# The first eight rows of both weights as a pipeline with one written order per engine

## The chip, the cores and the metric

The kernel runs on one core of one Trainium2 chip. The core has a tensor engine (PE; its weight loads are listed apart as PEld), a vector engine (DVE), a scalar engine (ACT), GpSimd (POOL) and a sync engine (SP) that issues the transfers here. The metric is the device time of one execution in microseconds; less is better.

## What is computed

Inputs are `x` (8 batches, 8 heads, 512 tokens, 64 features), `state` (8 batches, 8 heads, 32 slots, 64 features) and two weights of a feed-forward part, `w_in` (512 x 2048) and `w_out` (2048 x 512).

```python
scores  = scale * x @ state^T          # per batch and head, 512 x 32
a       = softmax(scores)              # over the 32 slots
xread   = a @ state
scores2 = scale * state @ x^T          # the same numbers, transposed
a2      = softmax(scores2)             # over the 512 tokens
sread   = a2 @ x
X       = concat(xread, sread)         # heads side by side: 4352 rows x 512
h       = X @ w_in
out     = (h - tanh(h)) @ w_out
```

The weights arrive as 64-bit floats (a block of 128 x 512 is 512 KB) and are turned into 32-bit floats on the chip by integer operations.

## The kernel before, in words

**What a chunk is.** A chunk is one batch's 512 token rows (chunk 8 is the 256 rows of `sread`). `xread` is never formed: for a batch `b` the kernel forms a product of the state with `w_in` (called `m`, 256 x 512 for each quarter `q` of the 2048 hidden columns), and a hidden row `f` (128 of the 2048 hidden columns) is `m` times the softmax weights `at`. There are 16 hidden rows per chunk. Each is followed by tanh (ACT, tile `t`), a subtraction (DVE), and a split of the result into two parts of reduced precision, high by an ACT cast and low by a DVE subtraction (tile `g`, L98 and L99, or L631 and L632 at the start). An output row adds the hidden row's share to the chunk's four output banks: 12 matmuls, high x high, high x low, low x high (L459 to L461). A hidden row takes two full-precision matmuls where `m` is not split (L417, two records each), else six of reduced precision (L419 to L421).

**The weights.** A block of `w_in` or `w_out` is loaded raw (L117) into one of five buffers (`parts` x 3 and `twins` x 2, taken in turn, L94), and converted in four steps (L128 to L132): a shift with a mask on DVE, a merge on DVE, a scaled copy of the low word on ACT, and an addition on DVE. `w_out` blocks are then split by ACT and DVE into the tile `wo` (L244). `w_in` is also written back to memory in 32 bits (`wf`, L519, L608) for the products of later batches. `load(n)` issues the next n loads of the list at L522; in most places it is called behind a conversion, which frees a buffer.

**Order of chunks.** Chunk 0 does its first 8 rows, then chunk 1 does all 16, then chunk 0 its last 8 (with the first half's sum kept in memory, `half`), then chunks 2 to 8. This is the list `steps`; the loop over it takes the hidden row two steps ahead (`LAG`), then the output row of the step itself. `SCH` says at which step a piece of conversion, of a product pair or of another batch's attention is put in.

**What sets the order on the engines.** At the start a written string, `SEQ`, gives one order for all engines: `D` blank matmuls, `S` scores, `c T M B E Z N A` the softmax of batch 0 (copy, transpose, maximum, subtraction, exp, sum with its reciprocal, multiplication, transpose back), `a r b p` the four conversion steps of a column block of `w_in`, `m` its product, `k` and `R` the copies of that product for batch 0 and batch 1, `h H` the two halves of a hidden row, `X` tanh with its subtraction, `G` the split. It covers the first quarter's four columns and two hidden rows. Everything behind that, from the second quarter of `w_in` (as four row blocks, products at L165) and the first `w_out` block on, is ordered by the compiler's own planner, which works from estimated times; `issue_after` gates hold a piece back until a given instruction has been issued.

**Banks and buffers.** PSUM has four output banks (`ps_o`), two for hidden rows (`ps_h`), two for products and scores (`ps_a`). `t` and `g` have three buffers each, `wor` and `cr` (converted block, scaled low word) two.

Of the kernel before, what the change touches and what calls it, by code (L numbers as in the profile page):

```python
# [19 lines left out]
P = 128  # L20
# [16 lines left out]
def attention_ffn(ctx: ExitStack, tc: tile.TileContext, xT, xn, bd, bh, sp, sm, sl, win, wout, xout, sout):  # L37
# [34 lines left out]
    wo = cpool.tile([P, NFF, 2, DM], F32R, name="wo")  # L72
# [21 lines left out]
    raws = itertools.cycle([parts] * PB + [twins] * 2)  # L94
# [6 lines left out]
    class Weight:  # L101
# [17 lines left out]
        def steps(self, dst):  # L119
# [5 lines left out]
            r = pool.tile([P, 512], I32, tag="cr", name=f"{self.name}r", bufs=CB)  # L125
# [115 lines left out]
    def convert_wout(f, part):  # L241
        w = pool.tile([P, 512], F32, tag="wor", name=f"wor{f}", bufs=RB)
        part.convert(w)
        split(wo[:, f, 0], wo[:, f, 1], w)  # L244


    def attention(b, aT):


        if b < LONE:  # L250
            bdr = pool.tile([P, 4, 64], F32, tag="bdr", name=f"bdr{b}", bufs=1)
        else:
            bdr = pool.tile([P, 4, NS], F32, tag="bdr", name=f"bdr{b}", bufs=1)
        with tc.issue_after(loadlog[min(len(loadlog) - 1, XH1)]):
            nc.sync.dma_start(bdr, bd[b] if b < LONE else bh[b - LONE])
# [7 lines left out]
        pss = {}  # L263

        def scores(hf):
            pss[hf] = bank(ps_a, f"sps{b}{hf}")
            for c in range(2):
                nc.tensor.matmul(pss[hf][64 * c : 64 * c + 64], bdr[:, 2 * hf + c], xrs[hf][:, c], start=True, stop=True)

        def all_scores():  # L270

            pss.update({hf: bank(ps_a, f"sps{b}{hf}") for hf in range(2)})
            for j in range(4):
                for hf in range(2):
                    rs = slice(64 * hf, 64 * hf + 64)
                    nc.tensor.matmul(  # L276
                        pss[hf][32 * j : 32 * j + 32], bdr[rs, j], xrs[j // 2][rs, j % 2], start=True, stop=True
                    )

        if b >= LONE:  # L280
            all_scores()
        for hf in range(2):
            if b < LONE:
                scores(hf)
            ps = pss[hf]
            s = pool.tile([P, 512], F32, tag=f"s{b}{hf}" if b < EARLY_S else "s", name=f"s{b}{hf}", bufs=1 if b < EARLY_S else 2)
            nc.scalar.copy(s, ps)
# [11 lines left out]
        for hf in range(2):  # L299
            e = es[hf]  # L300
            ef = e.rearrange("p a n -> p (a n)")
            z = pool.tile([P, 16, 1], F32, tag="z", name=f"z{b}{hf}")
            nc.vector.reduce_sum(z, e, axis=AX.X)
            nc.vector.tensor_scalar_add(z, z, EPS)
            nc.vector.reciprocal(z, z)
            nc.vector.tensor_mul(e, e, z.broadcast_to([P, 16, 32]))
            if b == 1:

                if hf == 0:
                    both = pool.tile([P, 2, 512], F32, tag="x", name="at1", bufs=XB)  # L310
                at = both[:, hf]
            else:
                at = pool.tile([P, 512], F32, tag="at", name=f"at{b}{hf}", bufs=1)
            nc.vector.transpose(at, ef)
            if b == 1:
                ats[1][hf] = at
            if b != 1:
                split(aT[:, 0, hf], aT[:, 1, hf], at)
            yield
        if b == 1:  # L320
            for hf in range(2):
                yield split(aT[:, 0, hf], aT[:, 1, hf], both[:, hf])
        if b >= EARLY_S:
            yield from state_read(b, ss)
        else:
            late[b] = ss

    late = {}

    def late_read(b):  # L330
        yield from state_read(b, late[b])

    def split_first():
        for hf in range(2):
            yield split(aTs[0][:, 0, hf], aTs[0][:, 1, hf], ats[0][hf])
# [57 lines left out]
    class Chunk:  # L393
# [38 lines left out]
        def output(self, f):  # L432
# [17 lines left out]
            if f == NFF - 1 or self.i == 0 and f == HALF - 1:  # L450
# [3 lines left out]
        def add(self, f, t):  # L454
# [4 lines left out]
            nc.tensor.matmul(o, g[:, 0, tok], wo[:, f, 0], start=first, stop=False)  # L459
            nc.tensor.matmul(o, g[:, 0, tok], wo[:, f, 1], start=False, stop=False)  # L460
            return nc.tensor.matmul(o, g[:, 1, tok], wo[:, f, 0], start=False, stop=last).ins  # L461

        def store(self, t, f):
# [15 lines left out]
            if t % 2 == 0:  # L479
# [15 lines left out]
    def advance(units, n=1):  # L495
# [12 lines left out]
    w0[0] = [  # L508
        Weight(win[:, j * P : j * P + P].rearrange("(r p) f -> p r f", p=P), f"w0{j}") for j in range(4)
    ]  # L510
# [3 lines left out]
    def convert_win(q, p):  # L514
# [18 lines left out]
    firstDVE = [None]  # L533

    def o(x):
        tc.keep_in_program_order(x)
        if x.ins.engine == mybir.EngineType.DVE:
            firstDVE[0] = x.ins

    aTs[0] = pool.tile([P, 2, 2, 512], F32R, tag="aT0", name="aT0", bufs=1)  # L540
    bdr = pool.tile([P, 4, 64], F32, tag="bdr", name="bdr0", bufs=1)
    sps = pool.tile([P, 4, P], F32, tag="sm", name="sps", bufs=1)
    xrs = [pool.tile([P, 2, 512], F32, tag="x", name=f"xT0{hf}", bufs=XB) for hf in range(2)]
    load(1)
# [8 lines left out]
    warm = bank(ps_a, "warm")  # L553
    m_first[0] = pool.tile([P, 2, 512], F32, tag="mr", name="mr00", bufs=RRB)
    wb, mps, sps_ps, hps, ss = {}, {}, {}, {}, {}
    es, ms, zs = {}, {}, {}
    csteps = {}
    hts = {}
    PING = int('0')
    tanhs = []  # L560
    nd = 0

    def e3(hf):
        return es[hf].rearrange("p (a n) -> p a n", n=32)

    def step(op):
        k, j = op[0], int(op[1]) if len(op) > 1 else 0
        if k == "D":
            o(nc.tensor.matmul(warm[:, :256], blank[:, :P], blank[:, :256], start=True, stop=True))  # L569
        elif k == "S":  # L570
            sps_ps[j] = bank(ps_o, f"sps0{j}")
            for c in range(2):
                o(nc.tensor.matmul(sps_ps[j][64 * c : 64 * c + 64], bdr[:, 2 * j + c], xrs[j][:, c], start=True, stop=True))
        elif k == "c":
            ss[j] = pool.tile([P, 512], F32, tag=f"s0{j}", name=f"s0{j}", bufs=1)
            o(nc.scalar.copy(ss[j], sps_ps[j]))
        elif k == "T":
            es[j] = pool.tile([P, 512], F32, tag="e", name=f"e0{j}")
            o(nc.vector.transpose(es[j], ss[j]))
        elif k == "M":  # L580
            ms[j] = pool.tile([P, 16, 1], F32, tag="m1", name=f"m10{j}")
            o(nc.vector.reduce_max(ms[j], e3(j), axis=AX.X))
        elif k in "Bq":
            o((nc.gpsimd if k == "q" else nc.vector).tensor_sub(e3(j), e3(j), ms[j].broadcast_to([P, 16, 32])))
        elif k == "E":
            o(nc.scalar.activation(es[j], es[j], AF.Exp, scale=SCALE))
        elif k == "Z":
            zs[j] = pool.tile([P, 16, 1], F32, tag="z", name=f"z0{j}")
            o(nc.vector.reduce_sum(zs[j], e3(j), axis=AX.X))
# [200 lines left out]
```

## Time and profile before

| | us |
|---|---|
| three runs | 669.41, 669.62, 669.88 (median 669.62) |
| span of the profiled execution | 669.9 |
| PE busy | 654.2 |
| PEld busy | 517.9 |
| DVE busy | 458.7 |
| ACT busy | 375.0 |
| POOL busy | 1.2 |

In the profile an instruction row gives its start and length in us, engine, line, operation, output and inputs, form and count, and in brackets the idle time before it with what ended it. Matmuls overlap: the length of one is longer than the distance to the next, so distances between starts, or the net lengths in the chain of waits, are what adds up. A full-precision matmul shows as two records. The granted clock is the share of full speed that PE's clock had. The records begin at 0.24 us with constants; the last transfer is issued at 666.59 us.

### The profile page before, as it was taken

Reading aid. Unit: us, or ns where it says so; the run is one execution under the profiler, and the core shown is the slowest. Engines: PE = TensorE matmul, PEld = TensorE weight load, DVE = VectorE, ACT = ScalarE, POOL = GpSimd, SP = SyncE. Lnnn points to the kernel's source line nnn. Section 1 sums busy time; section 2 is a strip of 40 time slices with the busy share of each in tenths; the row PEclk is TensorE's granted clock in tenths of the full one; section 3 lists DMA queues with packets and bytes.
Section 4 is the critical chain, followed back from the end, with each engine's and each line's share of the span. In section 5 each row is a group of like instructions: output and inputs, shape, how many; then the busy total and the mean of one; then the engine's idle time right before and its main releaser. Section 6 shows DMA issues by size and latency. Waiting matters only on the chain.

```text
span 669.9 us, 9418 instructions
## 1 busy us (share of the span) xinstructions
PE 654.2 (98%) x3452; PEld 517.9 (77%) x3452; DVE 458.7 (68%) x809; ACT 375.0 (56%) x665; POOL 1.2 (0%) x7
## 2 busy tenths in 40 slices
PE   7789999999999999999999999999999999999997
PEld 4446577887888878887888788887878788888996
DVE  5879898968856468667974589457864686444542
ACT  3676587867755555676755566544433454333442
POOL 0000000000000000000000000000000000000000
PEclk9889999999999999999999999999999999999999
DMA  9596485566556643455466145554151312010300
GB/s 317 155 307 225 159 296 207 177 189 205 185 173 205 173 160 113 140 166 149 134 218 165 55 152 182 174 169 145 54 193 42 126 64 95 1 32 29 130 31 32
DMA packets 45934, 99.25 MB, mean 148 GB/s; under 512 B 6080, under 2 KB 11456, under 8 KB 45888
## 3 DMA queue, kind: packets, MB, share of 16 engines
q1 hardware_dynamic: 45888, 98.65, 45.4%
q8 instruction: 27, 0.44, 0.3%
q14 instruction: 19, 0.16, 0.1%
HBM read 66.65 MB, written 31.98 MB: 147 GB/s over the span
## 4 chain that ended last, share of the span: by engine, by line
PE 95%; DVE 2%; ACT 1%; DMA 1%; issue 0%; POOL 0%; ACTq 0%; DVEq 0%; POOLq 0%
PE ops L459 19%; PE ops L460 18%; PE ops L461 18%; PE hps L419 9%; PE hps L420 9%; PE hps L421 9%; PE mps L201 2%; PE hps L417 2%; PE sps L276 1%; PE mps L165 1%; PE rps L369 1%; PE mps L200 1%; PE pps L356 1%; DMA wo2d<-in_wout 1%; PE warm L569 1%; PE hps L621 1%
## 5 line engine op out<-in xcount | busy, mean ns | idle before, releaser
L459 PE MATMUL ops<-wo,g 128*128 128x512 f32 x544 | 212.8, 395 | 2.0 <-ACT wo L98 2.0
L460 PE MATMUL ops<-wo,g 128*128 128x512 f32 x544 | 213.9, 393 | 0.0
L461 PE MATMUL ops<-wo,g 128*128 128x512 f32 x544 | 202.1, 394 | 0.0
L427 ACT ACTIVATE t<-hps 128x512 f32<-128x512 f32 (+1 forms) x142 | 81.1, 573 | 137.1 <-PE hps L421 131.7
L427 DVE TENSOR_TENSOR t<-hps,t 128x512 f32<-128x512 f32 (+1 forms) x142 | 93.0, 657 | 86.3 <-ACT t L427 85.7
L459 PEld LDWEIGHTS ops<-wo,g 128*128 128x128 f32 x544 | 102.0, 188 | 29.3 <-ACT wo L98 3.6
L99 DVE TENSOR_TENSOR g<-t,g 128x512 fp32r<-128x512 f32 (+1 forms) x142 | 93.0, 656 | 42.1 <-ACT g L98 39.6
L461 PEld LDWEIGHTS ops<-wo,g 128*128 128x128 f32 x544 | 102.1, 188 | 24.2 <-issue 2.8
L460 PEld LDWEIGHTS ops<-wo,g 128*128 128x128 f32 x544 | 102.2, 188 | 23.5 <-issue 3.4
L98 ACT CAST g<-t 128x512 fp32r<-128x512 f32 (+1 forms) x142 | 84.6, 597 | 63.2 <-DVE t L427 50.5
L419 PE MATMUL hps<-aT,m 128*128 128x512 f32 x232 | 91.6, 395 | 0.0
L420 PE MATMUL hps<-aT,m 128*128 128x512 f32 x232 | 90.8, 391 | 0.0
L421 PE MATMUL hps<-aT,m 128*128 128x512 f32 x232 | 90.4, 389 | 0.0
L99 DVE TENSOR_TENSOR wst<-w,wst 64x512 fp32r<-64x512 f32 x64 | 43.9, 686 | 12.3 <-ACT wst L98 10.2
L419 PEld LDWEIGHTS hps<-aT,m 128*128 128x128 f32 x232 | 43.6, 188 | 9.5 <-DVE g L99 0.2
L420 PEld LDWEIGHTS hps<-aT,m 128*128 128x128 f32 x232 | 43.6, 188 | 9.4 <-issue 0.5
L421 PEld LDWEIGHTS hps<-aT,m 128*128 128x128 f32 x232 | 43.6, 188 | 9.1
L202 ACT COPY st<-mps 128x512 f32<-128x512 f32 x64 | 36.6, 588 | 18.3 <-PE mps L201 18.0
L99 DVE TENSOR_TENSOR m<-mr,m 128x1024 fp32r<-128x1024 f32 x29 | 35.4, 1222 | 11.7 <-ACT m L98 8.5
L98 ACT CAST wst<-w 64x512 fp32r<-64x512 f32 x64 | 39.5, 617 | 0.8
L98 ACT CAST m<-mr 128x1024 fp32r<-128x1024 f32 x29 | 30.3, 1045 | 6.8 <-DMA mr<-md 6.7
L201 PE MATMUL mps<-wst,sms 128*128 128x512 f32 x64 | 24.5, 393 | 0.0
(216 smaller groups left out, 600.7 us busy)
## 6 DMA issues: line engine op xcount, KB each, us to landing
md<-st SPq DMA_DIRECT2D x128, 128.0 KB, 2.3
mr<-md SPq DMA_DIRECT2D x26, 512.0 KB, 3.8
xT<-in_xT SPq DMA_DIRECT2D x16, 512.0 KB, 5.3
w<-wf SPq DMA_DIRECT2D x16, 512.0 KB, 4.2
xn<-in_xn SPq DMA_DIRECT2D x16, 512.0 KB, 4.4
out_x<-ob SPq DMA_DIRECT2D x32, 256.0 KB, 2.3
wn<-wf SPq DMA_DIRECT2D x8, 512.0 KB, 3.8
ml<-md SPq DMA_DIRECT2D x8, 512.0 KB, 3.7
```

Of the source, the lines that this page charges most:

```text
L98: nc.scalar.copy(hi, src)
L99: return (sub or nc.vector).tensor_sub(lo, src, hi)
L201: nc.tensor.matmul(ps, s[:, 0, h], t[:, e], start=(g == 1), stop=True)
L202: nc.scalar.copy(stage[:, e], ps)
L417: nc.tensor.matmul(ps, mhi[k][:, cols], ats[i][k], start=(k == 0), stop=(k == 1))
L419: nc.tensor.matmul(ps, mhi[k][:, cols], ahi[:, k], start=(k == 0), stop=False)
L420: nc.tensor.matmul(ps, mhi[k][:, cols], alo[:, k], start=False, stop=False)
L421: nc.tensor.matmul(ps, mlo[k][:, cols], ahi[:, k], start=False, stop=(k == nk - 1))
L427: tanhs.append((nc.scalar.activation(t, ps, AF.Tanh).ins, nc.vector.tensor_sub(t, ps, t).ins))
L459: nc.tensor.matmul(o, g[:, 0, tok], wo[:, f, 0], start=first, stop=False)
L460: nc.tensor.matmul(o, g[:, 0, tok], wo[:, f, 1], start=False, stop=False)
L461: return nc.tensor.matmul(o, g[:, 1, tok], wo[:, f, 0], start=False, stop=last).ins
```

## The change

The prologue is rewritten. It now covers chunk 0's first eight hidden and output rows, eight columns of `w_in` (both first quarters as columns), the first eight blocks of `w_out`, both batches' softmax, and chunk 1's first two hidden rows.

- **Orders.** Three strings, one each for PE, DVE and ACT, fix the order of these pieces on each engine (`manual_schedule`); a loop emits each engine's next piece as soon as what it needs has been emitted. Letters as before; new ones are `I J` (add epsilon, reciprocal), `u v w y` (conversion of a `w_out` block), `i l` (its split), `L` and `g` (the two DVE subtractions), `O Q` (output row: first and last two of four banks), `V` (an output bank to memory).
- **Loads.** The first sixteen blocks each have a buffer: the five of the ring, eight `slots` (reused later by `wo` blocks 8 to 15), two halves of the tile `aT0`, and one of `m`. Two are issued between the small inputs, fourteen in one run. Batch 0's scores inputs go out first, and batch 1's go out at the start too.
- **Softmax of batch 0** is transposed straight from PSUM; the copy `c` remains for the later state read.
- **Stores** of chunk 0's first half are all copied by ACT; before, two of four were copied by DVE.
- **Behind the prologue** the loop begins at step 8. Conversions are gated by the tanh of the next row (`st + 1`) where before it was the row itself; `prepare` has such a gate too; the splits of `aT0` move from steps 9 and 10 to 11 and 13, those of `aT1` are both at step 9.

The diff's core (`win_step`, `product` and the like hold the operations that `step` held):

```diff
-    raws = itertools.cycle([parts] * PB + [twins] * 2)
+    ring = [parts] * PB + [twins] * 2
...
+    raws = itertools.chain(
+        ring, [slots] * (NFF // 2), [other("aT0", 1)] * 2, [other("m", MB)], itertools.cycle(ring)
+    )
...
-            if t % 2 == 0:
+            if t % 2 == 0 or i == 0:
                 nc.scalar.copy(ob, o)
...
+    wcols = w0[0] + w0[1]
     loads = iter(
-        w0[0] + wos[:1] + w0[1][:2] + w0[1][2:3] + wos[1:2] + w0[1][3:4] + wos[2:8] + w0[2][0:2]
+        wcols[:3] + wos[:1] + wcols[3:4] + wos[1:2] + wcols[4:5] + wos[2:3] + wcols[5:6]
+        + wos[3:4] + wcols[6:7] + wos[4:5] + wcols[7:8] + wos[5:8] + w0[2][0:2]
...
+    nc.sync.dma_start(bdr[:, :, 0:64], bd[0])
+    nc.sync.dma_start(xrs[0], xT[0, 0])
     load(1)
-    nc.sync.dma_start(bdr, bd[0])
+    nc.sync.dma_start(xrs[1], xT[0, 1])
+    nc.sync.dma_start(sps, sp)
+    load(1)
+    nc.sync.dma_start(bdr[:, :, 64:], bh[1 - LONE])
     for hf in range(2):
-        nc.sync.dma_start(xrs[hf], xT[0, hf])
-    nc.sync.dma_start(sps, sp)
-    load(4)
+        nc.sync.dma_start(xr1[:, hf], xT[1, hf])
+    load(14)
...
-    SEQ = 'D D D D D D a0 r0 b0 p0 S0 c0 T0 S1 D D M0 c1 B0 T1 E0 D D M1 B1 a1 r1 E1 b1 m0 k0 p1 Z0 N0 D A0 m1 k1 Z1 N1 D A1 a2 r2 h0 H0 h1 H1 b2 X0 p2 G0 X1 m2 a3 r3 b3 p3 D m3 k2 D G1 k3'
...
+    def turn(j):
+        es[j] = pool.tile([P, 512], F32, tag="e", name=f"e{j // 2}{j % 2}")
+        nc.vector.transpose(es[j], pss[j] if j < 2 else ss[j])
...
+    def wout_step(n):
+        def run(f):
+            if f not in wsteps:
+                worows[f] = pool.tile([P, 512], F32, tag="wor", name=f"wor{f}", bufs=RB)
+                wsteps[f] = wos[f].steps(worows[f], "s")
+            wsteps[f][n]()
+            if n == 3:
+                load(int(f < len(ring)))
+        return run
...
+    lines = {
+        "PE": (
+            "D0 D0 D0 D0 D0 D0 D0 D0 S0 D0 D0 D0 D0 D0 D0 S1 m0 D0 D0 D0 D0 D0 D0 D0 D0 D0 h0 S2 m1 H0 h1 H1 m2 O0 "
+            "h2 Q0 H2 O1 m3 Q1 h3 m4 H3 O2 h4 Q2 H4 O3 m5 Q3 h5 m6 H5 O4 h6 Q4 H6 O5 m7 Q5 h7 H7 O6 Q6 h8 h9 H8 H9 "
+            "O7 Q7"
+        ),
+        "DVE": (
+            "T0 a0 M0 b0 B0 p0 Z0 T1 I0 M1 J0 B1 a1 N0 Z1 A0 I1 b1 J1 p1 N1 A1 a2 b2 T2 u0 p2 v0 L0 y0 a3 g0 u1 l0 "
+            "v1 L1 y1 b3 g1 l1 u2 a4 v2 p3 y2 L2 b4 l2 p4 u3 g2 v3 u4 y3 a5 v4 L3 b5 l3 p5 g3 a6 y4 b6 L4 p6 l4 g4 "
+            "u5 a7 v5 b7 y5 p7 u6 M2 L5 l5 T3 g5 v6 B2 y6 L6 M3 l6 B3 Z2 g6 I2 u7 J2 Z3 N2 v7 I3 A2 J3 L7 N3 y7 A3 "
+            "g7 l7 L8 L9 g8 g9"
+        ),
+        "ACT": (
+            "c0 r0 E0 c1 k0 R0 r1 E1 r2 c2 k1 X0 w0 c3 R1 r3 G0 i0 X1 w1 k2 R2 r4 G1 i1 w2 X2 r5 i2 w3 k3 G2 R3 r6 "
+            "w4 k4 X3 i3 R4 G3 w5 r7 X4 i4 G4 k5 R5 w6 k6 R6 X5 i5 G5 w7 X6 E2 i6 G6 k7 R7 E3 X7 G7 i7 X8 X9 G8 V0 "
+            "V1 G9 V2 V3"
+        ),
+    }
...
+    with tc.manual_schedule(engines={mybir.EngineType.PE, mybir.EngineType.DVE, mybir.EngineType.Activation}):
+        while any(queues.values()):
+            moved = False
+            for e, l in queues.items():
+                while l and ready(l[0]):
+                    x = l.pop(0)
+                    ops[x[0]][0](int(x[1:]))
+                    done.add(x)
+                    moved = True
...
-    for st, (i, f) in enumerate(steps):
+    for st, (i, f) in list(enumerate(steps))[HALF:]:
         with ExitStack() as gates:
-            for x in tanhs[st] if st >= HALF else (first,):
+            for x in tanhs[st + (st < 2 * NFF)]:
                 gates.enter_context(tc.issue_after(x))
...
-            if st in [9, 10]:
+            if st == 9:
+                next(second_split)
+                next(second_split)
+            if st in [11, 13]:
                 next(first_split)
```

More of the change, by code (lines that the diff above doesn't have):

```diff
@@ L262, in attention @@
         yield
[L263 to L281, printed above, removed]
-        for hf in range(2):
[L283 to L287, printed above, removed]
+        pss = all_scores(b, bdr, xrs)
+        for hf in range(2):
+            s = pool.tile([P, 512], F32, tag="s", name=f"s{b}{hf}")
+            nc.scalar.copy(s, pss[hf])
             ss.append(s)
@@ L506, in attention_ffn @@
     ]
[L508 to L510 removed]
+    for q in range(2):
+        w0[q] = [
+            Weight(win[:, j * P : j * P + P].rearrange("(r p) f -> p r f", p=P), f"w0{j}")
+            for j in range(4 * q, 4 * q + 4)
+        ]
     wos = [Weight(wout[f * P : f * P + P], f"wo{f}") for f in range(NFF)]
@@ L552, in attention_ffn @@
     nc.gpsimd.memset(blank, 0.0)
[L553 removed]
+    warm = bank(ps_h, "warm")
     m_first[0] = pool.tile([P, 2, 512], F32, tag="mr", name="mr00", bufs=RRB)
[L555 to L559, printed above, removed]
[L560 to L597 removed]
@@ new lines, in attention_ffn, with rows, e3, blank_matmul @@
+    m_first[1] = pool.tile([P, 2, 512], F32, tag="m", name="mr01", bufs=MB)
+    for q in range(2):
+        m_second[q] = second(q)
+    wb, mps, pss, hps, ss, es, ms, zs, hts, worows = ({} for _ in range(10))
+    csteps, wsteps = {}, {}
+    tanhs = []
+    both = []
+    def rows(q, j):
+        return q[:, :, (j % 4) * P : (j % 4) * P + P]
+    def e3(j):
+        return es[j].rearrange("p (a n) -> p a n", n=32)
+    def blank_matmul(j):
+        nc.tensor.matmul(warm[:, :256], blank[:, :P], blank[:, :256], start=True, stop=True)
@@ new lines, in scores, with keep_scores @@
+    def scores(j):
+        if j < 2:
+            pss[j] = bank(ps_o, f"sps0{j}")
+            for c in range(2):
+                nc.tensor.matmul(pss[j][64 * c : 64 * c + 64], bdr[:, :, 0:64][:, 2 * j + c], xrs[j][:, c], start=True, stop=True)
+        else:
+            pss[2], pss[3] = all_scores(1, bdr[:, :, 64:], [xr1[:, hf] for hf in range(2)], ps_o)
+    def keep_scores(j):
+        ss[j] = pool.tile([P, 512], F32, tag=f"s{j // 2}{j % 2}", name=f"s{j // 2}{j % 2}", bufs=1)
+        nc.scalar.copy(ss[j], pss[j])
@@ new lines, in wout_high, with wout_low, product, keep_first @@
+    def wout_high(f):
+        nc.scalar.copy(wo[f][:, 0], worows[f])
+    def wout_low(f):
+        nc.vector.tensor_sub(wo[f][:, 1], worows[f], wo[f][:, 0])
+    def product(j):
+        w = wb[j // 2][:, j % 2].rearrange("p (r f) -> p r f", r=4)
+        mps[j] = bank(ps_a, f"mps0{j}").rearrange("p (r f) -> p r f", r=4)
+        for p in range(4):
+            nc.tensor.matmul(mps[j][:, p], sps[:, p], w[:, p], start=True, stop=True)
+    def keep_first(j):
+        for c in range(2):
+            nc.scalar.copy(rows(m_first[j // 4][64 * c : 64 * c + 64], j), mps[j][0:64, c::2])
@@ new lines, in keep_second, with hidden_half, run, tanh @@
+    def keep_second(j):
+        for c in range(2):
+            nc.scalar.copy(rows(m_second[j // 4][64 * c : 64 * c + 64], j), mps[j][64:128, c::2])
+    def hidden_half(k):
+        def run(n):
+            b, f = n // HALF, n % HALF
+            if k == 0:
+                hps[n] = bank(ps_h, f"hps{b}_{f}")
+            m = rows((m_first, m_second)[b][f // 4], f)
+            nc.tensor.matmul(hps[n], m[:, k], ats[b][k], start=(k == 0), stop=(k == 1))
+        return run
+    def tanh(n):
+        hts[n] = pool.tile([P, 512], F32, tag="t", name=f"t{n // HALF}_{n % HALF}", bufs=TB)
+        tanhs.append([nc.scalar.activation(hts[n], hps[n], AF.Tanh).ins])
@@ new lines, in attention_ffn, with ready @@
+    queues = {e: l.split() for e, l in lines.items()}
+    done = set()
+    def ready(x):
+        fn, before = ops[x[0]]
+        need = [c + x[1:] for c in before if not (c + x[1:] in SKIP)] + more.get(x, "").split()
+        return all(y in done for y in need)
+    SKIP = {"S3", "k8", "k9"}
+    with tc.manual_schedule(engines={mybir.EngineType.PE, mybir.EngineType.DVE, mybir.EngineType.Activation}):
[7 more added lines that the diff above has]
+                    moved = True
+            assert moved, {e: l[:3] for e, l in queues.items()}
```

258 lines of the change are left out of this document (134 added, 124 removed).

## The prediction

> **What bounds the kernel now.** First the totals, then stretches of the span (columns: stretch and length; busy PE, PEld, DVE, ACT, POOL with instructions; granted clock, DMA share, GB/s).
>
> ```profile
> span 669.9 us, 9418 instructions
> PE 654.2 (98%) x3452; PEld 517.9 (77%) x3452; DVE 458.7 (68%) x809; ACT 375.0 (56%) x665; POOL 1.2 (0%) x7
> ```
> ```profile
> 0.00:73.90 73.90, 63.34 (x228) 38.69 (x228) 59.54 (x108) 42.70 (x78) 1.17 (x7) 0.95 0.72 241
> 73.90:77.30 3.40, 1.98 (x4) 0.68 (x4) 3.40 (x8) 3.40 (x8) 0.00 (x0) 1.00 0.14 28
> 77.30:640.00 562.70, 562.68 (x3061) 455.41 (x3062) 385.41 (x674) 319.38 (x559) 0.00 (x0) 1.00 0.44 143
> ```
>
> From 77.3 to 640 us PE has no idle time at full clock. The end is therefore set by PE's work plus what PE loses before 77.3 and in the tail, which the change leaves alone. So I ask when PE has done the part that the new order covers: eight hidden rows and eight output rows of batch 0, eight products, both batches' scores, two hidden rows of batch 1.
>
> ```profile
> 70.30 3.59 PE L417 MATMUL hps<-at,mr 128*128 128x512 f32 x8
> 74.51 1.98 PE L417 MATMUL hps<-at,mr 128*128 128x512 f32 x4 [0.61 <-DVE t L427]
> 77.32 1.13 PE L417 MATMUL hps<-at,mr 128*128 128x512 f32 x2 [0.83 <-DVE t L427]
> 37.00 0.43 DVE L128 TENSOR_SCALAR wor<-wo2d 128x512 uint32<-128x512 uint32 x1 [2.27 <-DMA wo2d<-in_wout]
> 39.34 0.96 PE L459 MATMUL ops<-wo,g 128*128 128x512 f32 x3 [2.03 <-ACT wo L98]
> ```
>
> The x8 row is batch 1's first two hidden rows (four records each). It ends at 70.30 + 3.59 = **73.9 us**, and everything in the list is then done. Two bubbles of 0.61 and 0.83 follow, so PE is as far as if it had run without a gap from **75.3**. The last two rows are one loss inside the stretch: a weight block that landed late, then its conversion, then PE. What the list costs at PE's own pace comes from the chain of waits (net pitch) and the timeline:
>
> ```profile
> 52.43 1.72 PE hps L417 x4
> 66.83 0.91 PE ops L461 x4
> 30.55 1.05 PE L613 MATMUL mps<-w,sps 128*128 128x128 f32 x8
> 31.44 0.60 PE L569 MATMUL warm<-blank 128*128 128x256 f32 x2
> 54.85 1.02 PE sps L276 x16
> 6.56 1.08 PE L573 MATMUL sps<-xT,bdr 128*64 128x512 f32 x4
> ```
>
> A hidden row is 1.72, an output matmul 0.91/4 = 0.228, a product 31.44 - 30.55 = 0.89. So 10 x 1.72 + 96 x 0.228 + 8 x 0.89 + 2 x 1.08 + 1.02 = 49.4 us of 73.9: 24.5 us are blank matmuls, waits and half clock. That is all the change can win, plus the 1.4.
>
> **The change part by part.** No arithmetic goes away. The old rows of the second quarter of the first weight (four products, L165) become columns of as much data: taken at the same 0.89 (bounds 0.1 either way, on 4 x 0.89). Two output copies move from DVE to ACT. The rest is order and buffers, so the question is where the new orders end. DVE's pitches, from starts of neighbours:
>
> ```profile
> 61.58 0.68 DVE L427 TENSOR_TENSOR t<-hps,t 128x512 f32<-128x512 f32 x1
> 62.18 0.67 DVE L294 TENSOR_REDUCE m<-e 128x16 f32<-128x512 f32 x1
> 62.77 0.68 DVE L99 TENSOR_TENSOR wo<-wor,wo 128x512 fp32r<-128x512 f32 x1
> ```
> ```profile
> 23.31 0.42 DVE L128 TENSOR_SCALAR wor<-wo0d 128x512 uint32<-128x512 uint32 x1
> 23.65 0.42 DVE L128 TENSOR_SCALAR w<-w11d 128x512 uint32<-128x512 uint32 x1
> 67.57 0.29 DVE L304 TENSOR_SCALAR z<-z 128x16 f32<-128x16 f32 x2
> 68.06 1.29 DVE L306 TENSOR_TENSOR e<-e,z 128x512 f32<-128x512 f32 x2
> ```
> ```profile
> 1.46 5.17 PE L569 MATMUL warm<-blank 128*128 128x256 f32 x12 [1.46 <-POOL blank L552]
> 9.11 1.99 PE L569 MATMUL warm<-blank 128*128 128x256 f32 x8
> 8.30 0.71 DVE L579 STREAM_TRANSPOSE e<-s 128x512 f32<-128x512 f32 x1 [1.53 <-ACT s L576]
> 9.05 0.69 DVE L582 TENSOR_REDUCE m<-e 128x16 f32<-128x512 f32 x1
> 9.77 0.69 DVE L584 TENSOR_TENSOR e<-e,m 128x512 f32<-128x512 f32 x1
> ```
>
> Independent neighbours follow every 0.60 (the first three rows), the shift L128 every 0.34, and add-eps and reciprocal of two halves together take 0.49, say 0.12 each. Where each instruction needs the one before (8.30, 9.05, 9.77) it is 0.72 to 0.75.
>
> *Start.* Eight blank matmuls, 16 records, stand ahead of the first scores. Twelve took 5.17 (0.43 each, half speed), later ones 1.99/8 = 0.25. Four more put the scores at 7.4 (8.3 if the half speed lasts); they take 1.08, and DVE's first transpose, now straight from PSUM, starts at 8.5. Before it was 8.3, but with the first column's conversion already behind it: this end of the change costs.
>
> *DVE to the first output row.* From T0 to l0 the order has 24 large instructions, 6 shifts and 4 small ones: 24 x 0.60 + 6 x 0.34 + 0.5 = 16.9, plus 0.9 for its short waits on exp, the transposes and g. l0 is done at 26.3, and the first output matmul O0, which needs it, starts at **26.4**. PE has finished all that stands ahead of O0 by about 23.7, and its next products and hidden rows are queued behind O0: PE waits 2.7 us there.
>
> *PE from there.* 96 output matmuls x 0.228 = 21.9, eight hidden rows x 1.72 = 13.8, five products x 0.89 = 4.5: 40.1. DVE's work up to batch 1's last transpose A3 is 54 x 0.60 + 10 x 0.34 + 0.5 = 36.3, so it fits under PE with 4 us to spare until the end, where H8 waits 0.8 for A3; one more wait is 0.2. PE ends at 26.4 + 41.1 = **67.5**. After O0 PE is the bound, and any loss of PE there shows.
>
> ACT beside it:
>
> ```profile
> 22.10 0.75 ACT L643 COPY mr<-mps 64x256 f32<-64x256 f32 x2
> 28.33 0.62 ACT L631 CAST g<-t 128x512 fp32r<-128x512 f32 x1
> 28.85 0.61 ACT L98 CAST wo<-wor 128x512 fp32r<-128x512 f32 x1
> ```
>
> A pair of copies takes 0.75; a cast lets the next start after 28.85 - 28.33 = 0.52, and the others are put at up to 0.6. 16 pairs and 56 single instructions make about 44 us between 8 and 70: it never ends last for long. The moved output copies lie behind batch 1's first hidden rows, which cover them; uncovered they would be 2 x 0.6.
>
> *Clock.* O0's wait has a second price. The windows show it:
>
> ```profile
> 16.40:19.80 3.40, 1.32 (x3) 0.53 (x4) 3.26 (x7) 0.68 (x2) 0.00 (x0) 1.00 0.40 129
> 19.80:23.20 3.40, 3.40 (x5) 1.34 (x5) 1.82 (x4) 1.67 (x4) 0.00 (x0) 0.50 0.43 116
> 36.90:40.30 3.40, 1.37 (x5) 0.67 (x4) 3.30 (x6) 2.42 (x5) 0.00 (x0) 1.00 0.67 248
> 40.30:43.70 3.40, 3.40 (x6) 1.51 (x5) 3.40 (x7) 2.68 (x5) 0.00 (x0) 0.50 1.00 308
> ```
>
> Twice a 3.4 us stretch with PE busy 1.3 to 1.4 us is followed by 3.4 us at a granted 0.50; the stretch from 73.9, busy 1.98, is not. If these borders hold, the stretch 23.2 to 26.6 holds nearly all of the new wait (0.7 busy) and 26.6 to 30.0 runs at half: 1.7 us lost where PE is the bound. Bounds 0 (the wait falls astride a border) and 3.4 (a second such stretch); I take 1.7, which two stretches of this trace show. PE ends at 69.2. The Trainium skill, "TensorE: Matmul & The Clock Gate", Part 1 (the HAM clock gate), says the throttle comes back after at least one idle window of about 3.4 us. By that a 2.7 us wait costs nothing and the sum would be 1.7 lower; this trace shows half clock after windows that were not idle, so the row decides.
>
> *Loads.* Fourteen loads now go out in one run on SP's queue.
>
> ```profile
> w00d<-in_win SPq DMA_DIRECT2D x1, 512.0 KB, 4.0
> 10.00:15.00 5.00, 2.95 (x20) 2.42 (x19) 4.76 (x8) 2.44 (x5) 0.00 (x0) 1.00 1.06 381
> DMA packets 6607, 11.21 MB, mean 249 GB/s; under 512 B 384, under 2 KB 4608, under 8 KB 6605
> 6.01 1.67 SPq L117 DMA_DIRECT2D w10d<-in_win  x1
> ```
>
> The first 0.52 MB landed at 4.7 and the queue then moved 381 GB/s. With batch 1's inputs ahead, the first two blocks of the second weight end 4.65 and 5.70 MB into the queue: 15.5 and 18.3 us, needed at 21.5 and 25.3. The last block lands near 32 and is needed near 59. At the 249 GB/s mean of the first 45 us the tighter one lands at 25.5, 0.2 late. So cost 0 (bounds 0 and 0.2), and the 2.27 us landing wait goes. An issue can stall when many are under way (1.67 us); behind the loads stand only the write-backs of converted columns, first read in the rows after 100 us.
>
> *What is late next.* The new orders hand over from engine to engine some 0.05 us after each end, as the old rows do; at 0.1 the sum gains 0.6, so I add 0.3: **69.5**. After them the compiler's own schedule resumes, and DVE was full there before (next row).
>
> ```profile
> 80.00:100.00 20.00, 20.00 (x81) 14.60 (x79) 20.00 (x37) 15.94 (x29) 0.00 (x0) 1.00 0.83 269
> ```
>
> The splits of both batches' weights of attention, eight column conversions and the second weight's next blocks still lie there, so one of the old bubbles may stay: bounds 0 and 1.4, I take 0.7, the middle, since the new gates put conversions one row later and so behind the tanh work that then starved PE.
>
> *Sum.* 75.3 - 69.5 - 0.7 = 5.1 us. The profiled execution took 669.9, 0.3 over the 669.62 median of the runs, with nothing outside its span: 664.8 in its terms, **664.5** for the median.
>
> **Rivals.**
> 1. No half-clock stretch and no bubble. For: the wait is astride a border if the phase moves, and 1.4 us of idle at 73.9 was harmless. Against: with this trace's borders it falls inside one. 664.5 - 1.7 - 0.7 = 662.1, or 661 with faster hand-overs.
> 2. DVE becomes the bound at a middling pitch. At 0.66 the prelude is 1.4 longer and DVE needs 39.5 after it, then 4.5 for H8 to Q7: PE ends near 71.9. 75.3 - 71.9 - 0.7 = 2.7: 666.9. For: four long chains of softmax lie in this order. Against: their links are interleaved with conversions.
> 3. Slower: the same mechanism in full. If DVE's written order issues each large instruction only at the end of the one before, as at 8.30 to 9.77, the pitch is 0.72. End: 8.5 + 78 x 0.72 + 16 x 0.34 + 1.0 + 0.9 + 4.5 = 76.5, so 669.6 + (76.5 + 0.7 - 75.3) = 671.5. It beats the old kernel below a pitch of about 0.70. Against: nearly all neighbours are independent, and 61.58 to 62.77 hold 0.60.
> 4. It does what it says and gives it back. The conversions of the third and fourth quarters start one row later (gates of row st + 1) on a DVE that was full from 80 to 100. If PE then waits one row, 1.72 + 12 x 0.228 = 4.5 us, the time is 669.0. Against: those weights are due three rows after their conversion.
>
> **How the numbers follow.** Forecast 0.47, rival 1 0.19, rival 2 0.11, rival 4 0.11, rival 3 0.12. The forecast's own bounds (scores at 8.3: +0.9; bubble 0.7 more; no half clock: -1.7) give 662.5 to 666.5. The range must reach rival 1 and up to rival 4: 661.0 to 669.5. A measurement of this kernel can tell about 0.2%, 1.3 us. Faster takes the forecast and rivals 1 and 2, and a little of 4: 0.79; same is the rest of 4 and a mild case of 3: 0.09; slower 0.12.
>
> **What would show it.** Right: the first output matmul of batch 0 near 26.4 us, behind the cast's residue of the first second-weight block; one granted 0.50 stretch right after it; PE without gaps from there; batch 0's last early output matmul near 69 and not 70.3 with batch 1's two hidden rows before it; DVE large instructions at 0.60; no landing wait after 15 us. Wrong: the first transpose later than 9.5, DVE pitches near 0.7, a DMA named as releaser of the shifts L128, or PE idle between 75 and 120 us.

## The result

| | before | after |
|---|---|---|
| median of the timed executions | 669.75 us (4) | 666.38 us (4) |
| lowest to highest | 669.41 to 669.96 | 664.80 to 667.25 |
| span of the profiled execution | 669.9 | 665.4 |

The ratio is **0.9949, with a 95% interval of 0.9933 to 0.9965**: the change is worth 3.4 us, where 664.5 us (5.1 us less) was forecast. Run again on another occasion, the changed kernel took 666.51 us (ratio 0.9944, 0.9923 to 0.9965).

The totals of the changed kernel's page:

```profile
span 665.4 us, 9489 instructions
PE 656.3 (99%) x3494; PEld 523.5 (79%) x3494; DVE 455.4 (68%) x807; ACT 376.0 (57%) x675; POOL 1.2 (0%) x7
```

The same stretches as in the prediction, cut at the point where PE starts batch 1's third hidden row; the last three are around the first output row (stretch and length; busy PE, PEld, DVE, ACT, POOL; granted clock, DMA share, GB/s). After:

```profile
0.00:69.66 69.66, 65.36 (x271) 44.45 (x272) 57.91 (x110) 44.07 (x87) 1.17 (x7) 0.98 0.67 234
69.66:640.00 570.34, 569.15 (x3095) 459.89 (x3094) 389.76 (x681) 323.79 (x569) 0.00 (x0) 1.00 0.45 144
...
23.60:27.00 3.40, 1.61 (x10) 1.05 (x8) 2.94 (x6) 3.34 (x7) 0.00 (x0) 1.00 1.04 375
27.00:30.40 3.40, 3.17 (x7) 2.17 (x8) 3.12 (x6) 3.33 (x9) 0.00 (x0) 0.50 1.07 391
30.40:33.80 3.40, 3.40 (x14) 2.29 (x13) 3.23 (x7) 1.01 (x2) 0.00 (x0) 1.00 1.03 395
```

Before, cut at the same work:

```profile
0.00:74.51 74.51, 63.34 (x229) 38.70 (x229) 60.15 (x109) 43.31 (x79) 1.17 (x7) 0.95 0.72 240
74.51:640.00 565.49, 564.66 (x3065) 456.08 (x3066) 388.20 (x680) 322.18 (x564) 0.00 (x0) 1.00 0.44 142
```

The same work is done 74.51 - 69.66 = 4.85 us earlier, and PE's next bubble of 0.83 is gone too: a lead of 5.7. From there on the old kernel has only that bubble; the new one has 570.34 - 569.15 = 1.2 us of idle time. 5.7 - 1.2 = 4.5 us is what the two spans differ by. The timeline of the changed kernel carries the forecast's steps:

```profile
7.58 1.08 PE L566 MATMUL sps<-xT,bdr 128*64 128x512 f32 x4
8.71 0.72 DVE L576 STREAM_TRANSPOSE e<-sps 128x512 f32<-128x512 f32 x1 [8.71 <-PE sps L566]
...
23.66 1.05 PE L642 MATMUL mps<-w,sps 128*128 128x128 f32 x8
26.09 0.50 PE L448 MATMUL ops<-wo,g 128*128 128x512 f32 x1 [1.38 <-ACT wo L633]
27.23 0.79 PE L449 MATMUL ops<-wo,g 128*128 128x512 f32 x1 [0.64 <-DVE wo L636]
28.25 0.63 PE L448 MATMUL ops<-wo,g 128*128 128x512 f32 x1
28.68 0.63 PE L449 MATMUL ops<-wo,g 128*128 128x512 f32 x1
...
45.58 0.69 DVE L151 CUSTOM_DVE_ANT_0 w<-w,w06r 128x1024 uint16<-128x1024 uint16 x1
46.17 0.70 DVE L636 TENSOR_TENSOR wo<-wor,wo 128x512 fp32r<-128x512 f32 x1
46.78 0.69 DVE L675 TENSOR_TENSOR g<-t,g 128x512 fp32r<-128x512 f32 x1
...
65.06 1.98 PE L658 MATMUL hps<-at,mr 128*128 128x512 f32 x4 [0.46 <-DVE at L608]
69.43 0.39 PE L450 MATMUL ops<-wo,g 128*128 128x512 f32 x1
69.66 3.59 PE L406 MATMUL hps<-at,mr 128*128 128x512 f32 x8
```

Scores at 7.58, the first transpose at 8.71, the first output row at 26.09 behind the conversion of the first `w_out` block, then output matmuls 0.43 apart at half clock, DVE at 0.60 apart, H8's short wait for A3, and the last early output row at 69.43. The idle time behind the prologue is in two places (groups of PE from 77 to 640 us; the last column is the idle time before them and what ended it):

```profile
L408 PE MATMUL hps<-aT,m 128*128 128x512 f32 x232 | 91.7, 396 | 0.8 <-DVE t L416 0.8
L273 PE MATMUL sps<-xT,bdr 64*32 64x512 f32 x96 | 8.6, 601 | 0.4 <-DMA out_x<-ob 0.4
```

### The profile page after: what moved, and what is told of

The parts are those of the page before. It is cut to its first block, busy times and chain, and to the rows that moved or that the text cites. A ratio compares the mean times of both kernels' runs of the same rounds, so it can differ in the third digit from the quotient of the medians.

```text
span 665.4 us, 9489 instructions
## 1 busy us (share of the span) xinstructions
PE 656.3 (99%) x3494; PEld 523.5 (79%) x3494; DVE 455.4 (68%) x807; ACT 376.0 (57%) x675; POOL 1.2 (0%) x7
## 4 chain that ended last, share of the span: by engine, by line
PE 94%; DVE 4%; ACT 1%; DMA 0%; issue 0%; POOL 0%; ACTq 0%; POOLq 0%
PE ops L448 18%; PE ops L449 18%; PE ops L450 18%; PE hps L408 9%; PE hps L409 9%; PE hps L410 9%; PE mps L220 2%; PE warm L560 1%; PE rps L358 1%; PE hps L658 1%; PE sps L273 1%; PE mps L219 1%; PE pps L345 1%; PE mps L184 1%; PE mps L642 1%; PE hps L406 1%
## 5 line engine op out<-in xcount | busy, mean ns | idle before, releaser
L416 ACT ACTIVATE t<-hps 128x512 f32<-128x512 f32 (+1 forms) x134 | 76.4, 572 | 123.3 <-PE hps L410 122.6
L416 DVE TENSOR_TENSOR t<-hps,t 128x512 f32<-128x512 f32 (+1 forms) x134 | 87.3, 655 | 80.0 <-ACT t L416 79.3
L449 PEld LDWEIGHTS ops<-wo,g 128*128 128x128 f32 x544 | 102.5, 188 | 24.6 <-issue 2.8
L117 ACT CAST g<-t 128x512 fp32r<-128x512 f32 (+1 forms) x134 | 79.7, 596 | 58.8 <-DVE t L416 51.0
L118 DVE TENSOR_TENSOR g<-t,g 128x512 fp32r<-128x512 f32 (+1 forms) x134 | 87.5, 655 | 35.8 <-ACT g L117 34.3
L118 DVE TENSOR_TENSOR wst<-w,wst 64x512 fp32r<-64x512 f32 x64 | 43.9, 686 | 14.1 <-ACT wst L117 12.3
L118 DVE TENSOR_TENSOR m<-mr,m 128x1024 fp32r<-128x1024 f32 x29 | 35.4, 1222 | 15.6 <-ACT m L117 15.1
```

The lines of the kernel that those rows point to most:

```text
L117: nc.scalar.copy(hi, src)
L118: return (sub or nc.vector).tensor_sub(lo, src, hi)
L416: tanhs.append((nc.scalar.activation(t, ps, AF.Tanh).ins, nc.vector.tensor_sub(t, ps, t).ins))
L449: nc.tensor.matmul(o, g[:, 0, tok], wo[f][:, 1], start=False, stop=False)
```

## The experiments

The theory was that the **order** carries the gain. Its first rival was that the **buffers** do. A second question was what the **clock** costs. Ratios are against the kernel before, run beside each.

| | median us | ratio (95%) |
|---|---|---|
| changed kernel again | 666.51 | 0.9944 (0.9923 to 0.9965) |
| sixteen buffers, no written order | 674.83 | 1.0085 (1.0052 to 1.0117) |
| written order, old ring of five | 666.98 | 0.9967 (0.9938 to 0.9995) |
| kernel before with thirteen buffers | 670.50 | 1.0008 (0.9994 to 1.0022) |
| batch 1's softmax behind the rows | 672.76 | 1.0028 (1.0003 to 1.0053) |
| old gates behind the prologue | 668.18 | 0.9962 (0.9944 to 0.9979) |
| five blanks before the first output row | 666.09 | 0.9935 (0.9913 to 0.9956) |
| the same, six blanks at the start | 664.80 | 0.9916 (0.9897 to 0.9934) |
| five at the start, four before the row | 666.57 | 0.9947 (0.9930 to 0.9964) |
| kernel before with five more blanks | 669.80 | 1.0015 (1.0000 to 1.0029) |

### Without the written order

```diff
-    with tc.manual_schedule(engines={mybir.EngineType.PE, mybir.EngineType.DVE, mybir.EngineType.Activation}):
+    if True:
```

> The changed kernel with its sixteen buffered loads, but without the written order: the same pieces are emitted in the same sequence and the compiler's planner orders PE, DVE and ACT. Theory 'order' (the gain comes from the three written orders, which keep DVE at one large instruction per 0.6 us and PE without gaps after the first output row): the time goes back up, to 668.5 to 671 us, and the last output matmul of batch 0's first half comes later than 72 us. Theory 'buffers' (the gain comes from weights that have landed before they are needed; any order would use it): 665 to 667.5 us, as the changed kernel.

It took 674.83 us, beyond even what "order" expected. This run has no written order at all, not even the short one that the kernel before has at its start. PE's waits in its timeline:

```profile
20.33 1.13 PE L642 MATMUL mps<-w,sps 128*128 128x128 f32 x8 [1.88 <-DVE w L151]
25.12 2.05 PE L642 MATMUL mps<-w,sps 128*128 128x128 f32 x8 [3.66 <-DVE w L151]
33.36 1.98 PE L658 MATMUL hps<-at,mr 128*128 128x512 f32 x4 [1.87 <-DVE at L608]
38.90 1.40 PE L642 MATMUL mps<-w,sps 128*128 128x128 f32 x5 [2.21 <-DVE w L151]
42.61 0.79 PE L448 MATMUL ops<-wo,g 128*128 128x512 f32 x1
```

PE waits for conversions (`w`) again and again, and the first output row starts at 42.61 instead of 26.09. Buffers do not replace the order.

### The written order with the old ring

```diff
-    raws = itertools.chain(
-        ring, [slots] * (NFF // 2), [other("aT0", 1)] * 2, [other("m", MB)], itertools.cycle(ring)
-    )
+    raws = itertools.cycle(ring)
...
-    load(14)
+    load(3)
...
+    def release(x):
+        freed.add(x.name)
+        while issued[0] < 21 and order[issued[0] - len(ring)].name in freed:
+            load(1)
+            issued[0] += 1
```

> The changed kernel with its written orders, but with the old ring of five raw buffers: a load goes out only when the block that held its buffer has been converted. Followed through the order with 4 to 5 us from issue to landing, the fourth and fifth blocks of the second weight come 1.5 and 3 us late on DVE and the sixth column block about in time. Theory 'order': DVE has about 4 us to spare under PE, so of these some 1 to 3 us reach the end: 667.5 to 669.5 us, with a DMA named as releaser of the shift instructions. Theory 'buffers': the whole gain goes and more: 670 us or above.

666.98 us, under what both theories expected, and by its median not to be told from the changed kernel (the intervals overlap widely). DVE's longest waits up to 70 us:

```profile
DVE e L586 <- PE sps L576: 8.3, 1, 8.3
DVE t L677 <- ACT t L674: 1.1, 3, 0.7
```

No transfer is among them. The fourth block of the second weight, which I had 1.5 us late, in the view of its tile (instruction with its first and last start; time from issue to landing):

```profile
L136 SPq DMA_DIRECT2D wo3d<-in_wout x1: 340/340/340, 29.2 to 29.2; - x1
...
DMA to landing us min/median/max: 4.4/4.4/4.4
```

It goes out at 29.2, not at 33: its buffer is free when the merge has read it, and I had let it wait for the addition. It lands at 33.6, and the first to read it starts at 33.8. So **the sixteen buffers bring nothing inside the prologue that these runs can show**.

For the whole kernel this is less clear. Five of the six executions here had a granted clock of 0.999 or 1.000 and took 666.05 to 668.24 us; the five of the changed kernel at 1.000 (table under "The clock") took 664.80 to 665.95. At equal clock the old ring is thus 1.3 us slower by the medians (666.95 and 665.64). In its profile the prologue ends at 68.40, without a half-clock stretch and with the same waits of PE as in the changed kernel; behind it PE waits 1.0 us for a later batch's input. Whether the ring delays that transfer is not shown.

The written order came together with other parts, none of them taken out singly: the second quarter of the first weight as columns, the transposes straight from PSUM, the output copies on ACT, and the earlier issue of the inputs.

### The buffers alone

```diff
-    raws = itertools.cycle([parts] * PB + [twins] * 2)
+    ring = [parts] * PB + [twins] * 2
+    raws = itertools.chain(ring, [slots] * (NFF // 2), itertools.cycle(ring))
...
-    load(4)
+    load(12)
```

> The kernel before with one part of the change alone: thirteen of the first loads have buffers of their own (five of the ring and the eight slots), issued in one run, and later loads follow as ring buffers are freed; the planner still orders everything behind the short written start. Theory 'order': the 2.3 us landing wait at 37 us goes, but the planner's order and the half-clock stretches stay: 667.5 to 670 us (0 to 2 us faster than before). Theory 'buffers': the gain of the change is there: 665 to 667 us.

670.50 us: no gain at all, and above what both theories expected. The landing wait of 2.27 us is gone, but PE's longest waits in the first 75 us stay:

```profile
PE hps L426 <- ACT mr L629: 2.2, 1, 2.2
PE mps L626 <- DVE w L138: 2.2, 1, 2.2
```

They are for a copy and for a conversion, and the kernel before has the same two (2.1 and 2.0 us). Landed blocks do not remove them; in the changed kernel, with its written order, PE has neither.

### Batch 1's softmax behind the rows

On DVE the fifteen instructions from `M2` to `A3` move behind `g7`, on ACT `E2 E3` behind `G7`; PE does `O7 Q7` before `h8`.

```diff
-            "u5 a7 v5 b7 y5 p7 u6 M2 L5 l5 T3 g5 v6 B2 y6 L6 M3 l6 B3 Z2 g6 I2 u7 J2 Z3 N2 v7 I3 A2 J3 L7 N3 y7 A3 "
-            "g7 l7 L8 L9 g8 g9"
+            "u5 a7 v5 b7 y5 p7 u6 L5 l5 g5 v6 y6 L6 l6 g6 u7 v7 y7 L7 l7 g7 "
+            "M2 T3 B2 M3 B3 Z2 I2 J2 Z3 N2 I3 A2 J3 N3 A3 L8 L9 g8 g9"
```

> The changed kernel with batch 1's softmax (from its maxima on) put behind the eight rows on DVE and ACT instead of between them, and batch 1's first two hidden rows behind the last output row on PE. Theory 'DVE has spare time under PE between the rows, and the softmax chain is hidden there': its chain of some 9.5 us then stands bare behind the last output row, PE waits about 3.4 us for batch 1's first half and meets one more half-clock stretch, and the time is 669 to 671.5 us. Theory 'DVE is the bound and only the amount of work counts': the rows end as much earlier as the softmax ends later, and the time stays within 1 us of 666.4.

672.76 us. Its timeline and two stretches of PE (length, busy, granted clock):

```profile
69.67 6.68 PE L658 MATMUL hps<-at,mr 128*128 128x512 f32 x8 [3.43 <-DVE at L608]
76.63 3.70 PE L406 MATMUL hps<-at,mr 128*128 128x512 f32 x8 [0.28 <-DVE t L666]
```
```profile
68.87:72.28 3.41, 2.61 (x3) 0.50 0.00 0
72.28:75.70 3.42, 3.42 (x5) 0.50 0.00 0
```

The wait is the 3.4 us expected, but two half-clock stretches follow it and not one: two hidden rows that need 3.4 us take 6.7, and the third starts at 76.63 instead of 69.66. So the time is above both expected ranges. Between the rows the softmax lies under PE; behind them it costs 6.2 us of median, the most of all parts that were tried singly. Much of this is the clock: the two executions at a mean of 0.997 took 669.91, the four at 0.992 took 672.92 to 674.19.

### The gates

```diff
-            for x in tanhs[st + (st < 2 * NFF)]:
+            for x in tanhs[st]:
...
-                with ExitStack() as gates:
-                    for x in tanhs[st + 1] if st < 2 * NFF else ():
-                        gates.enter_context(tc.issue_after(x))
-                    chunks[ni].prepare(nf // 4)
+                chunks[ni].prepare(nf // 4)
```

> The changed kernel with the old gates behind the prologue: conversions of a row wait for that row's tanh and not the next row's, and the preparation of a chunk has no gate. Theory 'gates cost' (conversions one row late are what leaves PE two late gaps of 0.8 and 0.4 us): up to 1.2 us faster, 665.2 to 666.2. Theory 'gates protect' (without them conversions stand ahead of the tanh work again and PE gets the old bubbles of 0.6 and 0.8 us at steps 8 and 9): 0.6 to 1.4 us slower, 667 to 668.

668.18 us, just above what "gates protect" expected and 1.7 above the changed kernel beside it. The two intervals overlap, and both kernels spread with the clock; at a granted 1.000 the six executions here took 666.21 to 668.34 us, and all five of the changed kernel 664.80 to 665.95. Its timeline:

```profile
60.66 1.19 DVE L118 TENSOR_TENSOR m<-mr,m 128x1024 fp32r<-128x1024 f32 x1
62.61 1.12 PE L658 MATMUL hps<-at,mr 128*128 128x512 f32 x2 [0.69 <-DVE t L666]
196.89 0.50 PE L448 MATMUL ops<-wo,g 128*128 128x512 f32 x1 [2.38 <-DVE ob L459]
```

No bubble comes back at steps 8 and 9, but the reason given shows earlier, inside the prologue. The split of a batch's product that `prepare` brings (L118, 1.19 us) no longer waits for a gate and stands on DVE at 60.66, ahead of the tanh work; PE then waits 0.69 us for that work at 62.61. In the changed kernel this split comes at 77.61, and there is no such wait. A second loss, 2.38 us, stands at 197 us, where batch 0's second half is stored: PE waits for DVE, and DVE has waited 2.96 us for the transfer that brings `half` back. How the old gates lead to this one is not shown.

### The clock: blanks in the wait

The third product ends near 24.6 us and PE then waits for the first output row. Five blank matmuls fill the wait.

```diff
-            "... m2 O0 "
+            "... m2 W0 W0 W0 W0 W0 O0 "
...
+    def wait_matmul(j):
+        if 2 not in hps:
+            hps[2] = bank(ps_h, "hps0_2")
+        nc.tensor.matmul(hps[2][:, :256], blank[:, :P], blank[:, :256], start=True, stop=True)
```

> The changed kernel with five more blank matmuls (2.15 us at full clock) on PE between the third product and the first output row, where PE waits for the split of the first block of the second weight. Theory 'clock by activity' (a 3.4 us stretch with PE busy below about half is followed by 3.4 us at half clock, 1.7 us lost): the granted 0.50 near 26 us is gone in every execution, the mean granted clock is 1.000 in all of them, and the time is 664.5 to 665.8 us in all, where the changed kernel spreads from 664.8 to 667.25. Theory 'no cost' (PE makes the lost time up later, being bound by DVE): the stretch goes, but the median stays within 0.5 us of the changed kernel's 666.4.

666.09 us, all four executions between 665.33 and 666.11 at a granted clock of 0.999 or 1.000. The timeline:

```profile
24.60 2.32 PE L655 MATMUL hps<-blank 128*128 128x256 f32 x10
26.57 0.58 PE L448 MATMUL ops<-wo,g 128*128 128x512 f32 x1
27.32 0.50 PE L449 MATMUL ops<-wo,g 128*128 128x512 f32 x1 [0.15 <-DVE wo L636]
33.27 1.13 PE L642 MATMUL mps<-w,sps 128*128 128x128 f32 x8
68.73 3.59 PE L406 MATMUL hps<-at,mr 128*128 128x512 f32 x8
```

The half-clock stretch is gone, and the time is above the range of "clock by activity". The median gains 0.3 to 0.4 us, as "no cost" expected, and the two profiles show that this theory is right in part. The blanks let the row start 0.48 us later (26.57, not 26.09), but its second matmul, which waits for DVE in both, starts only 0.09 later (27.32, not 27.23). At the next hidden row PE is 1.37 us ahead of the changed kernel (the output matmul behind it starts at 29.05, not 30.42). At the fourth product it is 1.17 ahead (33.27, not 34.44) and at the fifth 0.98 (36.60, not 37.58): the fourth starts right behind its conversion on DVE (32.44 + 0.68 = 33.12), which ran without a pause from 29.95, and the hidden row before the fifth waits for a copy on ACT (34.87 + 0.72 = 35.59). The prologue ends 0.93 earlier (68.73, not 69.66).

> The changed kernel again, unedited, for its own spread beside the next three on one chip. If the half-clock stretch behind the first output row comes and goes with where the 3.4 us windows fall, executions divide into two groups, 664.7 to 665.8 us at a mean granted clock of 1.000 and 666.8 to 667.5 us at 0.997, with nothing between that has another clock. If the clock is not what divides them, times and clocks do not go together.

The changed kernel's ten executions of both occasions divide by clock, with three times a little outside the expected bounds (665.95, 667.55 and 668.70):

| mean granted clock | us |
|---|---|
| 1.000 | 664.80, 665.47, 665.64, 665.71, 665.95 |
| 0.997 | 667.08, 667.13, 667.25, 667.55, 668.70 |

The medians differ by 667.25 - 665.64 = 1.6 us, beside the forecast 1.7 for one stretch. By the clock, half of the executions have it. The traces of the prologue show less, some 0.9 to 1.0: from the first row's second matmul to H8 it is 37.83 us with the stretch (27.23 to 65.06), 36.82 with the five blanks (27.32 to 64.14) and 36.98 with the old ring (26.86 to 63.84). What makes up the rest of the 1.6 is not shown. The 668.70 lies above its group: its scores wait 1.8 us at a later batch, for a transfer (the profile names a store of `out_x`).

What brings the stretch is not the busy share alone. In the kernel before, a stretch busy for 1.59 us is followed by full clock (its next one, 16.4 to 19.8, stands at 1.00 in the prediction); so is one busy for 1.39 in the run with the old gates, which has the same waits ahead of the first output row (1.37 and 0.64):

```profile
13.00:16.40 3.40, 1.59 (x10) 1.00 1.05 392
```
```profile
23.60:27.00 3.40, 1.39 (x7) 1.00 1.06 380
27.00:30.40 3.40, 3.40 (x14) 1.00 1.06 387
```

Half clock begins at 19.83 and 40.31 us in the kernel before (6 x 3.41 apart), at 27.91 and 68.87 with the softmax behind the rows (12 x 3.41), at 26.97 and 27.38 in the two profiles of the changed kernel. So the stretches lie on a beat of 3.41 us that is the same all through one execution and shifted in another. With the old gates the row starts 0.76 us earlier (25.33, not 26.09), and where its wait falls on the beat may be what spares it half clock; the runs do not test this. It does not explain the stretch of 1.59, which lies on the beat of its own execution (19.83 - 2 x 3.41 = 13.0). What sets it apart from the one of 1.61 stays open.

### Six blanks at the start

The edit takes two `D0` from the eight ahead of `S0`, beside the five blanks above.

> The five blank matmuls before the first output row, and six blank matmuls instead of eight ahead of batch 0's first scores. Theory 'DVE's start sets all' (scores, first transpose, then DVE without a pause up to the first output row): the first transpose comes 0.9 us earlier, the first output row and all behind it too, and the time is 0.8 to 1 us under the kernel with the five blanks alone (666.09): 665.1 to 665.3. Theory 'the scores wait for their input': the scores start no earlier than the landing of batch 0's inputs, and the gain is under 0.3 us.

```profile
1.46 4.92 PE L560 MATMUL warm<-blank 128*128 128x256 f32 x12 [1.46 <-POOL blank L542]
6.31 1.08 PE L566 MATMUL sps<-xT,bdr 128*64 128x512 f32 x4
7.44 0.72 DVE L576 STREAM_TRANSPOSE e<-sps 128x512 f32<-128x512 f32 x1 [7.44 <-PE sps L566]
68.09 3.59 PE L406 MATMUL hps<-at,mr 128*128 128x512 f32 x8
```

**664.80 us, the lowest median here** (0.9916 of the kernel before). All five executions, 664.55 to 665.35, lie below the six of the changed kernel beside it (665.47 and more). The four with five blanks alone (665.33 to 666.11) were taken on another occasion and just touch them. Scores start at 6.31, 1.3 us earlier than with eight, so they do not wait for their input; half of that, 0.64, reaches the end of the prologue (68.09 against 68.73). Why only half is not shown.

### Five and four

> The changed kernel with five blank matmuls ahead of the first scores (eight before the edit) and four before the first output row. Against the kernel with six and five (664.80): if the scores can start right behind the fifth blank, the first transpose comes 0.4 us earlier, and the first output row 0.2 us less late: 664.2 to 664.5 us. If the input of the scores lands later than that, or the clock is not yet released after ten records, 664.8 us or more.

The prologue ends earlier still, and the median is 666.57:

```profile
67.34 3.59 PE L406 MATMUL hps<-at,mr 128*128 128x512 f32 x8
...
485.61 1.05 PE L273 MATMUL sps<-xT,bdr 64*32 64x512 f32 x4 [2.03 <-DMA xT<-in_xT]
```

0.75 us more of lead (though the first transpose starts at 7.37, only 0.07 earlier, and not the 0.4 expected), and 2.03 us lost at 486 us, where a later batch's scores wait for their input. The old kernel has no such wait, nor has the profile with six blanks; the changed one waits 0.4 here and 1.8 in the execution of 668.70. Two of the six executions, 664.54 and 665.39, are as fast as with six blanks. A lead won at the start can be lost to a transfer that is issued in the same place of the order; why it lands later in some executions stays open.

### The kernel before with blanks

```diff
-    SEQ = '... Z1 N1 D A1 a2 r2 h0 H0 ...'
+    SEQ = '... Z1 N1 D D D A1 a2 r2 h0 D D D H0 ...'
```

> The kernel before with five more blank matmuls on PE in its short written start (two before and three between the halves of the first hidden row), where PE waits for batch 0's two transposes; nothing else. Theory 'clock': the first half-clock stretch, near 20 us, goes, and the time falls by 1 to 1.7 us to 668 to 668.7 us; so part of what the change gains could be had without it. Theory 'order only': PE waits there anyway, so running slow costs nothing, and the time stays at 669.4 to 670.2 us.

669.80 us, no gain. PE's stretches (length, busy, granted clock):

```profile
17.29:20.70 3.41, 3.16 (x11) 1.00 0.27 88
20.70:24.12 3.42, 3.13 (x14) 1.00 0.45 143
24.12:27.53 3.41, 1.48 (x6) 1.00 0.49 145
27.53:30.95 3.42, 3.42 (x7) 0.50 0.78 251
```

The stretch at 20 us is gone, and another stands at 27.5 us behind the next wait (busy 1.48 of 3.41). One stretch took the place of another, so this run does not price the first one alone; it does show that five blanks at that place are not enough to give the old kernel any of the gain.

## Why the prediction was right, and by how much it was off

**The direction and the mechanism held**, and the time lies in the range; the size was put at 5.1 and is 3.4 us.

- *The start.* Forecast 7.4 for the scores and 8.5 for the first transpose; measured 7.58 and 8.71 (the rows used, 1.46 + 5.17 + 4 x 0.25, add up to 7.6, not 7.4). That this end of the change costs is confirmed by the run with six blanks.
- *DVE to the first output row.* Forecast 26.4, measured 26.09. The row's first matmul needs only ACT's high part; the second waits 0.64 more for DVE's low part at 27.23.
- *PE from there.* Forecast 67.5 without and 69.2 with one half-clock stretch, 69.5 with the hand-overs; PE was free for what follows at 69.66. It had no gap of note in between but the one for A3 (0.46 for 0.8 forecast).
- *The clock.* The stretch stands at 27.0 to 30.4 us, behind 1.61 us of busy time in 3.40. That it stands in the profiled execution is luck: the prediction took the borders of the old trace as fixed, and they shift from execution to execution. Rival 1, that it does not come, is what the other half of the executions do. Its price is 1.6 us by the two groups of executions and 0.9 to 1.0 by the traces of the prologue. So "any loss of PE there shows" held only in part: with five blanks some 0.4 us of the lead were lost again where PE waited for a conversion on DVE and a copy on ACT. The reading that 1.3 to 1.4 us of busy time in 3.4 bring half clock left out the stretch from 13.0 to 16.4 us. The Trainium skill, "TensorE: Matmul & The Clock Gate", Part 1, asks for an idle window before the throttle; no window here was idle, so the trace still speaks against that reading. What the Trainium skill says there of a free-running window fits the two groups.
- *Loads.* Cost 0 was right. The landing wait is gone with the old ring in the new order and with thirteen buffers in the old order: either is enough, and neither shows in the medians.
- *What is late next.* One bubble of 0.7 was put behind the prologue. At steps 8 and 9 there is none; 1.2 us come at 264 and 486 us instead.
- *Rivals 2 and 3* fall with DVE's starts at 45.58, 46.17 and 46.78. *Rival 4* is not borne out: with the old gates the kernel is slower, not faster.
- *The bounds.* The forecast's own bounds were added up wrong: its terms give 662.8 and 666.1, not 662.5 and 666.5. The stated range does not rest on this.

**The step that failed is the last line of the sum**: "The profiled execution took 669.9, 0.3 over the 669.62 median of the runs, with nothing outside its span". In every later execution for which both are given, the time is 1.7 to 1.9 us longer than the span (667.13 and 665.4 for the changed kernel's profiled one). So 669.9 of span is, by that, about 671.7 of time: that execution was some 2.0 us over the median, not 0.3 (its own time is not known). Its granted clock of 0.994 suggests why. Of 53 executions of the kernel before, on three occasions beside the experiments, 27 had 0.997 (median 669.41) and 9 had 0.994 (median 671.43). The profiled one had two half-clock stretches; a profile of this kernel with five blanks, at 0.997, has one, so one is what those 27 are likely to have. My sum compared two stretches before with one after and counted the difference as gain for the median.

In terms of spans the forecast was 669.9 - 5.1 = 664.8 and 665.4 was measured: 0.5 more of late gaps and 0.2 in the prologue. Add 1.7 outside the span, and take off 0.75, by which the changed kernel's profiled execution lies above its own median: 666.4.

How much of the 3.4 us is order and how much is clock can only be estimated. At an equal mean clock of 0.997 the medians are 669.41 before and 667.25 after, 2.2 us apart; the other 1.2 would come from the changed kernel meeting half clock less often.

## What to carry to other kernels

Where one engine is busy without a gap to the end, mark the same piece of work in both profiles and compare when that engine reaches it; the lead there, less the gaps behind it, is the change. Before summing from a profile, place that execution among the timed ones by its granted clock and by what lies outside its span. Here a chain of small dependent instructions cost 6.2 us less, half clock included, between the pieces of the bound engine's work than behind them. A wait that names a transfer does not by itself mean that buffers will pay: the kernel before had one of 2.27 us, and buffers removed it without any gain.

## What the runs showed of the hardware

- The same program meets the half-clock stretch in 5 of 10 executions (by the mean clock, 0.997 and 1.000), 1.6 us apart in the median. A stretch busy for 1.61 us of 3.40 came before it in one trace; one busy for 1.59 was followed by full clock in another.
- In one execution the half-clock stretches begin whole multiples of 3.41 us apart (20.48 and 40.96); from one execution to the next this beat is shifted.
- With blank matmuls in the wait it came in none of fifteen executions (three kernels, 0.999 or 1.000). Five of them ran 0.48 us past the row's first start, but the second matmul started only 0.09 later.
- An execution's time is 1.7 to 1.9 us longer than the span from first to last instruction.
- At one later batch PE's scores were held for 0.3 to 2.0 us by a transfer in some executions and not in others, with the same order of issue (the profile names the input's load or a store of `out_x`).
